# Two layers behind attention on one core: the tables of side work re-timed, product 5 ahead of the output pieces, weight fetches at a later unit, and an activation written with one relu

## The chip, the cores and the metric

The kernel runs on one core of a Trainium2 chip. A core has several engines, each with its own queue of instructions, taken strictly in order: TensorE (PE in the profile; PEld are its weight loads), VectorE (DVE), ScalarE (ACT), GpSimd (POOL) and SyncE (SP, which here only issues DMA transfers). Engines wait for one another by semaphores. The metric is the device time of one execution in microseconds (us).

## The reference

Causal attention with a decay feeds a feed-forward layer whose activation is h * relu6(h + 3) / 6, and that one a second layer whose activation is a PReLU with a slope per column:

```python
decay = cum[:, :, :, None] - cum[:, :, None, :]          # cum: running sum of log f
scores = where(causal, -1e9, scale * (q @ k.T) + decay)
attn = softmax(scores) @ v                                # 4 x 8 heads, 576 tokens, head width 64
x = attn as 2304 tokens x 512
h = x @ w_in;  g = h * clip(h + 3, 0, 6) / 6;  x = g @ w_out          # 512 -> 2048 -> 512
h = x @ w_in;  g = max(h, 0) + alpha * min(h, 0);  out = g @ w_out    # the same sizes
```

The weights reach the kernel as 64-bit words, and are converted to 32-bit floats on the chip.

## The kernel before

**Start and attention.** 32 heads are worked off as 16 pairs. For each head a tile of q and k (`rqk`) is loaded, prepared (`prep_head`, `prep_low`: high and low halves) and completed by four added rows that carry the decay. For the first two heads these rows are made in place; for the others they go through DRAM: `aq_d` and `ak_d` are stored once, and `prep_head` loads four rows of each (L313, L314). Attention runs to about 214 us. Beside it the weights of the first group are converted: `fetch` (L117) loads raw words, and the steps `m`, `f`, `s`, `j`, `g` (L137 to L153, ACT and DVE) make floats of them.

**The two layers.** The work is cut into 48 sets: two layers, in each 8 groups of 256 hidden columns by 3 blocks of 768 tokens. A set is a 2 x 2 block product done as in Strassen's and Winograd's schemes, with seven products (numbered 1 to 7) in place of eight. A product is six matmuls of 128 x 384 (high and low halves). Products accumulate in three PSUM banks: 1, 6, 7 and 4 one after another in bank A (tile `hA`), 5 and 3 in C (`hC`), 2 in B (`hB`). Behind products 1, 6 and 5 ACT copies the bank out (`keep`, L705); the next product of that bank must wait for it. Behind 3, 7 and 2 DVE adds the bank to such a copy (`add`, L708). Then `activate`: `first` on ACT (L663 in layer one; L666 and L668 in layer two), `second` on DVE (L674, L677), `third` a cast to the high half on ACT (L682) and the low half on POOL (L683). The activated blocks of a set are multiplied by the second weight matrix in the *pieces* (L731 in layer one, L733 in layer two), which run during the next set; DVE or ACT adds a piece's result (L740, L751, L738, L749).

**The order.** `run` walks a string for each set: a digit is a product, `q` one piece of the set before. Each character is a *unit*, and all engines' instructions are written out in the order of units: what `later` puts down for a unit comes right behind its matmuls, then what `aside` puts down. Side work has due units: `conversion` reads a table of names and units (`S1` to `S4` are sums of weight blocks on POOL, L167; `ha` to `hd` and `ho` casts on ACT, L181; `la` to `ld` and `lo` low halves on POOL, L185), and `build` makes the input blocks of the next sets (sums L237, casts L240, low halves L245), evenly spread if a rate is given.

Of the kernel before, what the change touches and what calls it, by code (L numbers as in the profile page):

```python
# [8 lines left out]
F32 = mybir.dt.float32  # L9
# [12 lines left out]
def decay_attention_ffn2_kernel(ctx, tc, qk, v, f, wi1, wo1, wi2, wo2, alpha, out):  # L22
# [28 lines left out]
    CONV_EVEN = "m0 0 f0 1 s0 2 j0 3.5 g0 5 m1 4 f1 6.5 s1 8 j1 9 g1 10 S1 11 S2 12 S3 12 hc 13 ha 13 lc 14 hb 14 la 15 lb 16 S4 17 m2 18 hd 18 f2 19 ld 19 s2 20 j2 21 m3 21 g2 22.5 f3 23 ho0 23 lo0 24 s3 24.5 j3 26 g3 27 ho1 28 lo1 29 wi0 40 wi1 43 wo0 46 wo1 48"  # L51
    CONV_TURN = "p0 0 p1 0 S1 6 S2 7 S3 7 hc 8 ha 8 lc 9 hb 9 la 10 lb 11 S4 12 hd 13 ld 14 p2 14 p3 15 ho0 24 lo0 25 ho1 26 lo1 27 wi0 40 wi1 43 wo0 46 wo1 48"
# [225 lines left out]
    def attention():  # L278
        with ExitStack() as ax:
# [219 lines left out]
            aug_consts(1)  # L499
            make_identity(nc, identb)  # L500
# [3 lines left out]
            nc.gpsimd.memset(aq.bitcast(F32)[:, :, 512:640], 0.0)  # L504
            nc.gpsimd.memset(aq.bitcast(F32)[:, 2:4, 0:512], -1.0)
            nc.gpsimd.memset(ak[:, 0:2, :].bitcast(F32), 1.0)
# [15 lines left out]
            prep_head(1)  # L522
            prep_low(1)
# [3 lines left out]
            for a in range(2):  # L527
                nc.gpsimd.affine_select(out=maskj[64 * a:64 * a + 64], in_=maskj[64 * a:64 * a + 64],
                                        pattern=[[-1, TAIL]], compare_op=ALU.is_ge,
                                        fill=-1.0e9, base=0, channel_multiplier=1)  # L530
            scaled("P", aq[:, 0:2, 0:512], hl[:, :, 0:512].bitcast(F32))
# [5 lines left out]
            nc.gpsimd.tensor_scalar(out=alpha_sb, in0=alpha_sb, scalar1=-1.0, scalar2=None, op0=ALU.mult)  # L537
# [9 lines left out]
            def aside(t, *fns):  # L547
                side.setdefault(t, []).extend(fns)

            aside(2, lambda: fetch(0), lambda: fetch(1))  # L550
# [64 lines left out]
    SEQ = ("1qq5q6q3q7q2q4q", "1q5q6q3q7q2q4")  # L615
    FIRST = ("152637..4", "15qq6qq3q7q2q4q", "1qq5qq6q3q7q2q4")
# [37 lines left out]
    def activate(s, gt, i, n, h, d):  # L654
# [5 lines left out]
        def first():  # L660
# [6 lines left out]
            hold["g"] = g32 = P["tp"].tile([128, NB], F32, tag="t", name="t") if (i, n) == (1, 0) else h()  # L667
            nc.scalar.activation(out=g32, in_=h(), func=AF.Relu)  # L668
            hold["t"] = t

        def second():
# [3 lines left out]
            else:  # L675
                m = g * FT + i
                nc.vector.scalar_tensor_tensor(out=g32, in0=hold["t"], scalar=alpha_sb[:, m:m + 1], in1=g32,  # L677
# [11 lines left out]
    def product(s, c, gt, k):  # L689
# [24 lines left out]
        else:  # L714
            k2, i, n = {2: (1, 0, 0), 7: (5, 1, 1), 3: (6, 0, 1)}[k]
            later(0, lambda: add(k2))
# [40 lines left out]
    def side_work(s):  # L757
# [13 lines left out]
        if s == (0, 1, 0):  # L771
            conversion(early["first"], CONV_FIRST, True)
            build(1, 1, both, even=(1, 1.5))
        if s == (0, 0, 1):
            ops = conv_ops(0, 2)
            conversion(ops, CONV_A, True, 1, 1)
# [126 lines left out]
```

## Time and profile before

| what | value |
|---|---|
| runs | 1013.03 us median of 3 (1013.02 to 1017.4) |
| profiled execution, its own time | 1012.13 us |
| its span | 1010.3 us |
| PE busy | 965.5 us, 96% of the span, 5488 matmuls |
| DVE, ACT, POOL busy | 735.9, 589.1, 590.0 us |

The span is what the profiler saw of that execution; the time of the execution is 1.8 us more. Busy shares are means over parts with different limits, so the stretch in question is looked at below, and the waits of PE.

### The profile page before, as it was taken

The page shows a single profiled execution, that of the slowest core. Times are in us where ns is not written, and L with a number is a line of the kernel's source. Part 1 is how long each engine was busy: PE and PEld are TensorE (multiplying, and loading weights), DVE is VectorE, ACT ScalarE, POOL GpSimd, SP SyncE. Part 2 cuts the span into 40 slices and gives each one's busy share as a digit, 9 for nine tenths or more (in the row PEclk, how much of TensorE's full clock was granted, in tenths as well). Part 3 has the DMA queues.
Part 4 walks back from the last instruction along what each step waited for, and adds up shares of the span by engine and source line. Part 5 has one row for each costly group of instructions (what it writes and reads, how often), then busy time and mean ns, then how long its engine had stood idle before and what let it go on. Part 6 is the DMA issues. An engine that isn't in the chain of part 4 may idle for free.

```text
span 1010.3 us, 15919 instructions
## 1 busy us (share of the span) xinstructions
PE 965.5 (96%) x5488; PEld 859.7 (85%) x5488; DVE 735.9 (73%) x1284; ACT 589.1 (58%) x1444; POOL 590.0 (58%) x577
## 2 busy tenths in 40 slices
PE   4999999999999999999999989999999999999998
PEld 3767666678899999998998988789898888898997
DVE  6888988857698788878989846145687788735454
ACT  5677787776555555555654445665565656564452
POOL 8567568956646666566485269566556556532222
PEclk9999999999999999999999999999999999999999
DMA  6555576501424444310576851332344420243531
GB/s 219 174 173 168 176 239 208 150 2 42 156 66 177 178 175 169 107 48 1 198 308 241 308 184 48 137 129 81 125 160 168 166 84 1 104 182 142 229 150 68
DMA packets 36868, 147.57 MB, mean 146 GB/s; under 512 B 4668, under 2 KB 4668, under 8 KB 33652
## 3 DMA queue, kind: packets, MB, share of 16 engines
q1 hardware_dynamic: 36784, 146.56, 41.7%
q8 instruction: 43, 0.70, 0.3%
q14 instruction: 37, 0.30, 0.1%
q10 hardware_dynamic: 4, 0.00, 0.0%
HBM read 98.26 MB, written 44.14 MB: 141 GB/s over the span
## 4 chain that ended last, share of the span: by engine, by line
PE 57%; DVE 23%; POOL 7%; ACT 6%; issue 4%; DMA 2%; SPq 0%; POOLq 0%; ACTq 0%; DVEq 0%
PE o L733 13%; PE hA L700 12%; PE o L731 12%; PE hC L700 7%; PE pv L454 4%; PE hB L700 3%; DVE nm L341 3%; PE tp L397 2%; DVE t L674 2%; PE sc L364 2%; POOL wi L185 2%; POOL g L683 1%; DVE r L751 1%; DVE s L708 1%; ACT g L682 1%
## 5 line engine op out<-in xcount | busy, mean ns | idle before, releaser
L731 PE MATMUL o<-g,wo 128*128 128x384 f32 x1152 | 233.3, 341 | 2.0 <-POOL g L683 2.0
L700 PE MATMUL hA<-xh,wi 128*128 128x384 f32 x768 | 225.8, 339 | 9.0 <-ACT s L705 5.4
L733 PE MATMUL o<-wo,g 128*128 128x512 f32 x864 | 225.5, 395 | 4.0 <-POOL g L683 3.0
L683 POOL TENSOR_TENSOR g<-t,g 128x384 fp32r<-128x384 f32 x120 | 128.8, 1073 | 156.1 <-ACT g L682 134.6
L731 PEld LDWEIGHTS o<-g,wo 128*128 128x128 f32 x1152 | 205.6, 189 | 4.6 <-POOL g L683 3.3
L733 PEld LDWEIGHTS o<-wo,g 128*128 128x128 f32 x864 | 159.8, 188 | 33.2 <-POOL g L683 6.2
L683 POOL TENSOR_TENSOR g<-s,g 128x384 fp32r<-128x384 f32 x72 | 74.7, 1038 | 155.6 <-ACT g L682 153.8
L700 PEld LDWEIGHTS hA<-xh,wi 128*128 128x128 f32 x768 | 142.0, 188 | 15.1 <-ACT s L705 7.6
L751 DVE TENSOR_TENSOR r<-o,r 128x512 f32<-128x512 f32 x126 | 86.2, 687 | 73.8 <-PE o L733 73.7
L700 PE MATMUL hA<-xl,wi 128*128 128x384 f32 x384 | 129.7, 338 | 0.0
L682 ACT CAST g<-t 128x384 fp32r<-128x384 f32 x120 | 61.9, 515 | 113.0 <-DVE t L674 97.3
L700 PE MATMUL hC<-xh,wi 128*128 128x384 f32 x384 | 115.0, 340 | 3.6 <-ACT s L705 3.6
L740 DVE SCALAR_TENSOR_TENSOR r<-o,r 128x384 f32<-128x384 f32 x168 | 90.6, 549 | 21.2 <-PE o L731 21.0
L349 ACT ACTIVATE p<-sc,nm 128x128 f32<-128x128 f32 (+4 forms) x160 | 84.6, 532 | 22.9 <-DVE nm L341 10.9
L245 POOL TENSOR_TENSOR xl<-r,xh 128x384 fp32r<-128x384 f32 x65 | 78.5, 1225 | 4.1 <-ACT xh L240 3.7
L341 DVE TENSOR_REDUCE nm<-sc 128x1 f32<-128x128 f32 (+4 forms) x160 | 71.7, 470 | 10.1 <-PE sc L366 8.5
L700 PEld LDWEIGHTS hC<-xh,wi 128*128 128x128 f32 x384 | 71.3, 189 | 6.7 <-ACT s L705 4.6
L700 PEld LDWEIGHTS hA<-xl,wi 128*128 128x128 f32 x384 | 72.4, 189 | 3.1
L682 ACT CAST g<-s 128x384 fp32r<-128x384 f32 x72 | 37.1, 515 | 60.1 <-DVE s L677 53.4
L397 PE MATMUL tp<-ident,p 128*128 128x128 f32 x384 | 68.6, 282 | 0.6 <-ACT pt L413 0.6
L364 PE MATMUL sc<-k,q 128*128 128x256 f32 (+2 forms) x128 | 55.6, 434 | 11.9 <-DVE k L332 9.8
L700 PE MATMUL hC<-xl,wi 128*128 128x384 f32 x192 | 65.1, 339 | 0.0
(128 smaller groups left out, 1901.8 us busy)
## 6 DMA issues: line engine op xcount, KB each, us to landing
wid<-wi SPq DMA_DIRECT2D x24, 896.0 KB
wi<-wid SPq DMA_DIRECT2D x12, 1792.0 KB
rqk<-in_qk SPq DMA_DIRECT2D x32, 608.0 KB
raw<-in_wi SPq DMA_DIRECT2D x32, 512.0 KB
raw<-in_wo SPq DMA_DIRECT2D x32, 512.0 KB
wod<-wo SPq DMA_DIRECT2D x24, 512.0 KB
wo<-wod SPq DMA_DIRECT2D x12, 1024.0 KB
vt<-in_v SPq DMA_DIRECT2D x16, 320.0 KB
```

What stands on the lines that cost most here:

```text
L245: e.tensor_sub(out=XS[k][1][:, b, c], in0=x, in1=XS[k][0][:, b, c].bitcast(F32))
L341: nc.vector.tensor_reduce(out=nm[:, i:i + 1], in_=src, axis=AX.X, op=ALU.max, negate=True)
L349: nc.scalar.activation(out=pt[:, c0:c0 + cw], in_=src, func=AF.Exp, bias=nm[:, 0:1], scale=1.0, accum_out=dsts[i])
L364: nc.tensor.matmul(out=sc[:, 0:n], lhsT=q1[:, qs], rhs=k1[:, 0:n], start=True, stop=False)
L397: nc.tensor.transpose(tp[:, j, :], pt[:, 128 * j:128 * j + 128], ident)
L682: nc.scalar.copy(out=gt[n][i][:, 0], in_=hold["g"])
L683: nc.gpsimd.tensor_sub(out=gt[n][i][:, 1], in0=hold["g"], in1=gt[n][i][:, 0].bitcast(F32))
L700: nc.tensor.matmul(out=h, lhsT=a, rhs=b[:, x, kc], start=new and kc + e == 0, stop=kc == KH - 1 and e == 2, skip_group_check=not new)
L731: nc.tensor.matmul(out=o[:, 0:NB], lhsT=a[:, cs], rhs=b, start=st, stop=sp)
L733: nc.tensor.matmul(out=o, lhsT=b[:, cs], rhs=a, start=st, stop=sp)
L740: later(0, lambda: nc.vector.scalar_tensor_tensor(out=acc, in0=o[:, 0:NB], scalar=1.0 / 6.0, in1=acc, op0=ALU.mult, op1=ALU.add))
L751: nc.vector.tensor_add(out=acc, in0=o, in1=acc)
```

## The change

It has six parts. The tables `CONV_EVEN` and `CONV_TURN` get other units (the cast `hb`, which needs no sum, first, the other casts behind the sums they read), and the set (0, 0, 1) uses `CONV_EVEN` stretched by 1.1 instead of two other tables. At the start three memsets are written earlier and the preparation of head 1 later. The first two raw fetches move from unit 2 of the attention to units 8 and 10. In the strings product 5 comes in front of the output pieces that follow product 1. `add` goes to the front of its unit's list, ahead of activations. In layer two `first` makes only relu(-h), and `second` computes h + (1 - alpha) * relu(-h), which is the same function; `alpha_sb` holds 1 - alpha.

```diff
-    CONV_EVEN = "m0 0 f0 1 s0 2 j0 3.5 g0 5 m1 4 f1 6.5 s1 8 j1 9 g1 10 S1 11 S2 12 S3 12 hc 13 ha 13 lc 14 hb 14 la 15 lb 16 S4 17 m2 18 hd 18 f2 19 ld 19 s2 20 j2 21 m3 21 g2 22.5 f3 23 ho0 23 lo0 24 s3 24.5 j3 26 g3 27 ho1 28 lo1 29 wi0 40 wi1 43 wo0 46 wo1 48"
-    CONV_TURN = "p0 0 p1 0 S1 6 S2 7 S3 7 hc 8 ha 8 lc 9 hb 9 la 10 lb 11 S4 12 hd 13 ld 14 p2 14 p3 15 ho0 24 lo0 25 ho1 26 lo1 27 wi0 40 wi1 43 wo0 46 wo1 48"
+    CONV_EVEN = "m0 0 f0 1.5 s0 2.5 j0 4 g0 5 m1 4 f1 6.5 s1 8 j1 9 g1 10 S1 11 S2 12 S3 13 hb 13 hc 14.5 lb 15 ha 15.5 lc 16 la 17 S4 18 m2 19 hd 20 f2 20.5 ld 21 s2 21.5 j2 22.5 m3 22 g2 23.5 f3 24 s3 25 ho0 25.5 j3 26.5 lo0 27 g3 27.5 ho1 28.8 lo1 29.6 wi0 40 wi1 43 wo0 46 wo1 48"
+    CONV_TURN = "p0 0 p1 0 S1 5 S2 6 S3 7 hb 8 hc 9 lb 10 ha 10.5 lc 11 la 12 S4 13 hd 15 p2 15 ld 16 p3 18 ho0 24 lo0 25.5 ho1 26 lo1 27 wi0 40 wi1 43 wo0 46 wo1 48"
...
+            nc.gpsimd.memset(aq.bitcast(F32)[:, :, 512:640], 0.0)
+            nc.gpsimd.memset(aq.bitcast(F32)[:, 2:4, 0:512], -1.0)
+            nc.gpsimd.memset(ak[:, 0:2, :].bitcast(F32), 1.0)
             make_identity(nc, identb)
...
-            nc.gpsimd.memset(aq.bitcast(F32)[:, :, 512:640], 0.0)
-            nc.gpsimd.memset(aq.bitcast(F32)[:, 2:4, 0:512], -1.0)
-            nc.gpsimd.memset(ak[:, 0:2, :].bitcast(F32), 1.0)
...
             load_head(3)
-            prep_head(1)
-            prep_low(1)
             nc.gpsimd.memset(three, 3.0)
...
+            prep_head(1)
+            prep_low(1)
             scaled("P", aq[:, 0:2, 0:512], hl[:, :, 0:512].bitcast(F32))
...
-            nc.gpsimd.tensor_scalar(out=alpha_sb, in0=alpha_sb, scalar1=-1.0, scalar2=None, op0=ALU.mult)
+            nc.gpsimd.tensor_scalar(out=alpha_sb, in0=alpha_sb, scalar1=-1.0, scalar2=1.0, op0=ALU.mult, op1=ALU.add)
...
-            aside(2, lambda: fetch(0), lambda: fetch(1))
+            aside(8, lambda: fetch(0))
+            aside(10, lambda: fetch(1))
...
-    SEQ = ("1qq5q6q3q7q2q4q", "1q5q6q3q7q2q4")
-    FIRST = ("152637..4", "15qq6qq3q7q2q4q", "1qq5qq6q3q7q2q4")
+    SEQ = ("15qq6qq3q7q2q4q", "15q6qq3q7q2q4")
+    FIRST = ("152637..4", "15qq6qq3q7q2q4q", "1qqqq5q6qq372q4")
...
             nc.scalar.activation(out=t, in_=h(), func=AF.Relu, scale=-1.0)
-            hold["g"] = g32 = P["tp"].tile([128, NB], F32, tag="t", name="t") if (i, n) == (1, 0) else h()
-            nc.scalar.activation(out=g32, in_=h(), func=AF.Relu)
-            hold["t"] = t
+            hold["g"] = t
...
-                nc.vector.scalar_tensor_tensor(out=g32, in0=hold["t"], scalar=alpha_sb[:, m:m + 1], in1=g32,
+                nc.vector.scalar_tensor_tensor(out=g32, in0=g32, scalar=alpha_sb[:, m:m + 1], in1=h(),
                                                op0=ALU.mult, op1=ALU.add)
...
-            later(0, lambda: add(k2))
+            at.setdefault(now[0], []).insert(0, lambda: add(k2))
...
-            build(1, 1, both, even=(1, 1.5))
+            build(1, 1, both, even=(1, 1.3))
...
-            conversion(ops, CONV_A, True, 1, 1)
-            conversion(ops, CONV_B, True, 1, 4, 0, 25)
-            conversion(ops, CONV_B, True, 1, 7, 25)
+            conversion(ops, CONV_EVEN, True, 1.1, 2)
```

Three places show how the order of instructions moves. A row names the line, the operation, what is written and what is read.

SP at the start, the difference of the two orders: `aq_d` is the store of the added rows of q, `raw` the raw weight words, the tiles `q_` and `k_` the added rows of heads 2 and 3, `rqk` and `vt` the loads of head 4.

```order
 L536 DMA aq_d<-aq 16x2560 x2
-L117 DMA raw<-in_wi 128x512 x2
-L313 DMA q_279<-aq_d 4x640
-L314 DMA k_281<-ak_d 4x576
-L313 DMA q_345<-aq_d 4x640
-L314 DMA k_347<-ak_d 4x576
-L295 DMA rqk<-in_qk 128x1216
-L300 DMA vt<-in_v 128x640
+L313 DMA q_275<-aq_d 4x640
+L314 DMA k_277<-ak_d 4x576
...
+L300 DMA vt<-in_v 128x640
+L117 DMA raw<-in_wi 128x512 x2
```

The two raw fetches stand behind the rows of heads 2 and 3 and the loads of head 4.

DVE in the second set of layer one, before: `hC`, `hA` and `hB` are the sums behind products 3, 7 and 2.

```order
L148 SCALAR_TENSOR_TENSOR wb<-raw,wb 128x512
L153 SCALAR_TENSOR_TENSOR wb<-raw,wb 128x512
L245 TENSOR_TENSOR xl_3592<-r_81,xh_3591 128x384
L708 TENSOR_TENSOR s<-hC,s 128x384
L245 TENSOR_TENSOR xl_3592<-r_81,xh_3591 128x384
L674 SCALAR_TENSOR_TENSOR t<-t,s 128x384
L708 TENSOR_TENSOR s<-hA,s 128x384
L237 TENSOR_TENSOR r_81<-r_81 128x384 x3
L674 SCALAR_TENSOR_TENSOR t<-t,s 128x384
L708 TENSOR_TENSOR s<-hB,s 128x384
```

The same place in the changed kernel, where `add` is on L707 and `second` on L673:

```order
L148 SCALAR_TENSOR_TENSOR wb<-raw,wb 128x512
L153 SCALAR_TENSOR_TENSOR wb<-raw,wb 128x512
L245 TENSOR_TENSOR xl_3592<-r_81,xh_3591 128x384
L707 TENSOR_TENSOR s<-hC,s 128x384
L707 TENSOR_TENSOR s<-hA,s 128x384
L673 SCALAR_TENSOR_TENSOR t<-t,s 128x384
L245 TENSOR_TENSOR xl_3592<-r_81,xh_3591 128x384
L237 TENSOR_TENSOR r_81<-r_81 128x384
L707 TENSOR_TENSOR s<-hB,s 128x384
L673 SCALAR_TENSOR_TENSOR t<-t,s 128x384
```

The sum of `hA` moved ahead of a low half (L245) and an activation.

ACT in the last set of layer one, before: the tiles `wi` are casts of the first weights of layer two, `xh_` those of input blocks, and L705 the copies.

```order
L705 COPY s<-hA 128x384
L181 CAST wi<-wc 128x2x256
L181 CAST wi<-wa 128x2x256
L181 CAST wi<-wb 128x2x256
L240 CAST xh_78<-r_81 128x384 x2
L705 COPY s<-hC 128x384
L705 COPY s<-hA 128x384
```

The same place in the changed kernel, with the copies on L704:

```order
L704 COPY s<-hA 128x384
L181 CAST wi<-wb 128x2x256
L704 COPY s<-hC 128x384
L181 CAST wi<-wc 128x2x256
L181 CAST wi<-wa 128x2x256
L240 CAST xh_78<-r_81 128x384 x2
L704 COPY s<-hA 128x384
```

The copy of product 5 moved ahead of two casts that read POOL's sums and of the two input casts; the cast of `wb`, which reads no sum, moved to the front.

## Rows read from the trace of the kernel before

**Rows 1.** PE's waits, whole span: engine, line, releaser: us in total, times, longest.

```profile
PE sc L365 <- DMA k<-ak_d: 3.9, 1, 3.9
```

**Rows 2.** PE's waits from 236 to 265 us.

```profile
PE hA L700 <- DVE s L708: 2.1, 1, 2.1
PE hA L700 <- ACT g L682: 1.4, 1, 1.4
```

**Rows 3.** PE's waits from 265 to 592 us.

```profile
PE hA L700 <- ACT s L705: 2.2, 2, 1.6
PE o L731 <- POOL g L683: 2.0, 4, 0.6
```

**Rows 4.** PE's waits from 592 to 640 us.

```profile
PE hC L700 <- ACT s L705: 3.1, 2, 2.6
PE hA L700 <- ACT s L705: 2.9, 3, 1.3
PE o L733 <- POOL g L683: 1.2, 1, 1.2
```

**Rows 5.** Groups of instructions, 645 to 1000 us: busy, mean ns, idle before and releasers.

```profile
L733 PE MATMUL o<-wo,g 128*128 128x512 f32 x802 | 210.0, 395 | 2.8 <-POOL g L683 1.8 <-ACT g L682 1.0
```

**Rows 6.** Busy time by stretch: PE, PEld, DVE, ACT, POOL, clock, DMA share, GB/s.

```profile
240.00:245.00 5.00, 2.90 (x14) 2.58 (x13) 4.88 (x6) 2.45 (x6) 3.45 (x3) 0.88 0.33 105
245.00:250.00 5.00, 5.00 (x24) 5.00 (x23) 3.64 (x7) 3.38 (x8) 2.42 (x3) 0.78 0.00 0
...
240.00:265.00 25.00, 21.49 (x113) 20.88 (x112) 22.52 (x35) 13.32 (x29) 15.38 (x13) 0.93 0.13 44
300.00:350.00 50.00, 50.00 (x287) 50.00 (x286) 40.28 (x72) 27.00 (x53) 33.78 (x33) 1.00 0.49 179
592.00:640.50 48.50, 41.27 (x211) 38.21 (x210) 22.81 (x37) 26.05 (x55) 44.33 (x42) 0.96 0.18 64
```

**Rows 7.** Timeline of the start: start, us, engine, line, idle before and releaser.

```profile
0.74 0.59 SPq L471 DMA_DIRECT2D fl<-in_f  x1
...
3.35 1.39 DVE L507 TENSOR_SCALAR fl<-fl 64x576 f32<-64x576 f32 x1 [0.18 <-DMA fl<-in_f]
...
16.34 2.86 SPq L117 DMA_DIRECT2D raw<-in_wi  x2
...
20.73 0.29 SPq L314 DMA_DIRECT2D k<-ak_d  x1
...
25.06 0.35 PE L365 MATMUL sc<-k,q 68*128 68x256 f32 x1 [3.86 <-DMA k<-ak_d]
```

**Rows 8.** Timeline of DVE ahead of the wait at 243 us.

```profile
241.39 1.34 DVE L674 SCALAR_TENSOR_TENSOR t<-t,s 128x384 f32<-128x384 f32 x1
242.66 0.55 DVE L708 TENSOR_TENSOR s<-hA,s 128x384 f32<-128x384 f32 x1
```

**Rows 9.** Copy of product 1 and first matmul of product 6, two sets.

```profile
285.93 0.47 ACT L705 COPY s<-hA 128x384 f32<-128x384 f32 x1
...
286.52 0.37 PE L700 MATMUL hA<-xh,wi 128*128 128x384 f32 x1
...
526.38 0.47 ACT L705 COPY s<-hA 128x384 f32<-128x384 f32 x1
...
527.71 0.34 PE L700 MATMUL hA<-xh,wi 128*128 128x384 f32 x1
```

**Rows 10.** Timeline from 592 us: POOL's first weight sum, ACT's first weight cast.

```profile
592.96 0.74 POOL L167 TENSOR_TENSOR wc<-wa,wb 128x256 f32<-128x256 f32 x1 [3.88 <-issue]
...
595.41 0.62 ACT L181 CAST wi<-wc 128x512 fp32r<-128x512 f32 x1 [5.37 <-POOL wc L167]
```

**Rows 11.** Timeline of one set of layer two: second relu, copy, product 6.

```profile
772.88 0.53 ACT L668 ACTIVATE s<-s 128x384 f32<-128x384 f32 x1
...
775.81 0.49 ACT L705 COPY s<-hA 128x384 f32<-128x384 f32 x1
...
777.06 0.34 PE L700 MATMUL hA<-xh,wi 128*128 128x384 f32 x1
```

## The prediction

> **What bounds the kernel now.** I read the busy times by stretch first. In a plain stretch of layer one, 300 to 350 us, PE is busy for 50.00 of 50 us with 287 instructions, which is 0.174 us a matmul and 1.05 us for a product or a piece of six; DVE does 40.28 there, ACT 27.00 and POOL 33.78 [rows 6]. So PE sets the pace, and the change, which takes no matmul away, can win only where PE stands still. I therefore went to the list of what PE waits for, first over the whole span and then by stretch. The reader is to see five places. At the start one wait of 3.9 us for the DMA that brings the added rows of k for the second head [rows 1]. Between 236 and 265 us, the second and third set of layer one, two waits of 2.1 and 1.4 us [rows 2]. Between 265 and 592 us, 20 sets, small ones: 2.2 us for copies of bank A and 2.0 us for the low halves that POOL makes for the output pieces [rows 3]. Between 592 and 640 us, where layer two begins, 3.1, 2.9 and 1.2 us [rows 4]. After that 2.8 us in all before output pieces, over some 22 sets [rows 5].
>
> A long wait costs twice. After the 2.1 us wait the granted clock of 240 to 245 us is 0.88 and of 245 to 250 us 0.78: 0.12 and 0.22 of 5 us, 1.7 us lost at the lower level (1.2 GHz). Over all of 240 to 265 us it is 0.93, which is 1.75 us lost, so nothing more was lost after the 1.4 us wait [rows 6]. A wait of 1.4 us left the clock alone here, and one of 2.1 us did not; where between them it turns these rows don't say. From 592 to 640.5 us it is 0.96, 1.9 us lost, which I put to the longest wait there, 2.6 us [rows 4, 6]. I charge 1.7 us to each of the waits of 3.9, 2.1 and 2.6 us.
>
> **Start.** PE stops at 21.20 us (25.06 less 3.86) and goes on when the rows of k have landed. SP issued them at 20.73 us, 4.3 us earlier, behind two raw fetches of 512 KB each, issued from 16.34 us on [rows 7]. The change puts these fetches behind the rows of q and k. A small transfer that nothing stood ahead of, fl at 0.74 us, was there for DVE at 3.35 us, 2.6 us later [rows 7]. So k lands at 23.3 us instead of 25.0, and the wait becomes 2.1 us: **-1.7 us**. That is the length after which the clock fell at 243 us, so I take no clock back. The bounds: nothing, if heads 2 and 3 fill the queues anyway, and -5.6 us (3.86 and the clock). The moved memsets and the first head's preparation change the order on POOL, but not the sum of what stands ahead of the store of aq there; so I leave that store's landing, which SP waits for before it issues the rows, where it is.
>
> The Trainium skill, page "DMA: Bandwidth & Descriptors", section "Anatomy of one DMA — SWDGE (gpsimd) path", gives a transfer a fixed cost of about 2.0 us whatever its size, on another issuing path than this one. By that rule (an estimate) the rows would land at 22.7 us, the wait would be 1.5 us and next to the 1.4 us after which the clock stayed, and this term would be -4.0 us. The trace has 2.6 us for 144 KB, and goes before it.
>
> **Second and third set.** PE's 2.1 us wait there is for the sum of product 7 on DVE, which started only at 242.66 us [rows 8], although its product was done before the piece ahead of the wait: it stood behind a low half (L245) and an activation (L674, at 241.39 for 1.34 us). In the change each sum stands at the head of its unit's list, and the even build is spread wider, so this sum follows the sum before it directly, and the low half and the activation come behind it; in the third set the join (L148) and the activation also give way. Both waits then go, 3.5 us, with 1.7 us of clock: 5.2 us at most. But DVE is busy for 22.52 of these 25 us [rows 6]. It cannot be compressed by more than the 2.5 us that it idles, except for work that slips behind 265 us, where it has room (40.28 of 50); I allow 1 us for that. **-3.5 us**, bounds -1.8 (the first wait is only shortened) and -5.2.
>
> **Remaining sets of layer one.** With product 5 ahead of the output pieces, the order 1, piece, piece, 5, piece, 6 becomes 1, 5, piece, piece, 6. A piece gets 1.05 us more for its low half to arrive, and all four waits of this kind (longest 0.6) go: -2.0 us. But product 6, which accumulates into bank A after product 1 has been copied out by ACT, comes one unit earlier after product 1. How much the copy leads was read set by set. In the tightest case the copy ends at 286.40 (285.93 and 0.47) and product 6 starts at 286.52, a lead of 0.12; in the last of six such sets it is 0.86 [rows 9]. In these six of 20 the lead is less than 1.05, and what is short adds up to 2.3 us. In the two sets where PE already waits for this copy (2.2 us, [rows 3]) the wait grows by a full unit each, 2.1 us. That is 4.4 us less 2.0. The sums in front bring the activations and casts ahead of the copy a little forward in some of them; I take **+2.0 us**, bounds -1 (copies all come earlier) and +4.5 (the piece waits had other causes).
>
> **Where layer two begins.** POOL is busy for 44.33 of the 48.5 us from 592 us [rows 6]. Its first sum of the new weights (L167) starts at 592.96 us with 3.88 us of idle time before it; ACT stands 5.37 us until POOL's second sum lets it cast at 595.41 us [rows 10], and behind three such casts stands the copy of product 5 for which PE waits 2.6 us. In the change one cast that needs no sum goes first, then that copy, then the others: this wait goes, with its clock 4.3 us, and the rest of [rows 4] is 4.6 us, so at most 8.9. But the weights are needed all the same, and POOL idles for only 4.2 us in that stretch, which is what this can shrink by unless POOL's work falls behind. I take **-3.0 us**, bounds 0 and -8.9.
>
> **Rest of layer two.** One ACT instruction of 0.53 us goes in each activation; DVE keeps its instruction, with h in place of the second relu as an input, so I cost it the same. Where the sum h comes straight from the PSUM bank the instruction reads PSUM, as the sums on DVE already do. Piece waits (2.8 us) go, as a product of 1.05 us comes in front of them. Here too product 6 moves up, by one piece. In the tight sets the copy, at 775.81 us, ends 0.76 before product 6 at 777.06 us; two of the removed instructions, one at 772.88 us of 0.53 us, stand ahead of it [rows 11], so that it moves up by 1.0 and product 6 by about 1.4: 0.4 of lead remain. I take **-2.5 us**, bounds 0 (the shorter ACT queue only idles and new copy waits eat the rest) and -2.8.
>
> **The sum.** -1.7 - 3.5 + 2.0 - 3.0 - 2.5 = -8.7 us. The profiled execution took 1012.13 us, the median of the runs is 0.9 us above that (1013.03), so 1003.4 becomes 1004.3; I say 1004.
>
> **Rivals.** *Slower: the sums in front hold DVE up.* A sum now waits at the head of DVE's queue for its product to end, and an activation of the unit before, which was ready, waits behind it; its cast, low half and piece follow late. With half a microsecond in each of the 38 sets without a wait that is +19 us, so 1023. It decides against the change from 0.18 us a set (8.7 over 48 sets). Against it: DVE has 9.7 us idle in 50 [rows 6], and pieces get 1.05 us more cover. Chance 0.08.
>
> *POOL gives it back.* The gain at 592 us comes out at nothing, since POOL ends its sums and low halves no earlier, and the copies in layer one cost their full 4.5: 1012.13 - 1.7 - 3.5 + 4.5 - 2.5 and the 0.9 is 1009.8; with only one of the two, 1007. For it: POOL's 44.33 of 48.5. Chance 0.20, of which 0.12 for a time within 0.5% of before.
>
> *The start does not change.* The heads' loads, not the raw fetches, keep the rows of k till 25 us: 1006. Chance 0.10.
>
> *Everything pays.* All waits and clock losses go (5.6, 5.2, 8.9, 2.8) and the copies cost nothing: 1012.13 - 22.5 + 0.9 is 990.5. With half of what lies between it and the sum, 997. Chance 0.15.
>
> The forecast itself has 0.47. A measurement of this kernel can tell about 0.5% (5 us) from no change. Faster by more: 0.47, 0.15, 0.10 and 0.08 of POOL's 0.20, 0.80; within it 0.12; slower 0.08. The range goes from between the two sizes of "everything pays", 994, to the worse of the POOL case, 1010.
>
> **What would show it.** Right: the wait for k at 21 us is 2.1 us and still followed by a low clock; no wait for a sum of product 7 at 243 us and a clock of 1.00 there; no 2.6 us wait at 598 us; no waits ahead of pieces, and more or longer waits of product 6 for ACT copies in layer one. Wrong: new waits in the plain sets (PE under 50 of 50 between 300 and 350 us), POOL behind at 640 us with waits that moved to its low halves, or an attention part that ends no earlier although its start did.

## The result, and the profile after

The changed kernel is slower: 1025.01 us median (1023.91 to 1026.77, 4 runs) against 1014.07 us (the three runs of before and a fourth), a ratio of 1.0104 (95% interval 1.0073 to 1.0134). The forecast was 1004 us. The profiled execution took 1025.94 us and its span is 1024.2 us, 13.9 us longer than that of before.

The parts of the two spans say where. The table takes the starts of the first matmul of product 1 of a set from the traces (sets numbered from 0; 24 begins layer two), and the difference of two starts is the length of a part:

| us | attention, to set 0 | sets 0 to 3 | 4 to 22 | 23 to 25 | 26 to 40 | rest |
|---|---|---|---|---|---|---|
| before | 214.5 | 66.7 | 307.0 | 57.7 | 241.6 | 122.7 |
| changed | 214.2 | 66.0 | 318.4 | 59.9 | 242.8 | 122.9 |
| difference | -0.4 | -0.7 | +11.4 | +2.2 | +1.2 | +0.2 |

Nearly all of the loss lies in the plain sets of layer one. PE's waits there, from 265 to 592 us, changed kernel (in total, times, longest):

```profile
PE hA L699 <- ACT s L704: 11.5, 11, 2.7
PE o L730 <- POOL g L682: 1.0, 2, 0.8
PE o L730 <- ACT g L681: 0.7, 1, 0.7
```

Against [rows 3] the waits for ACT's copies of bank A rose from 2.2 us in two places to 11.5 us in eleven; the waits ahead of pieces went from 2.0 to 1.7 us. Busy time by stretch, with the columns of [rows 6], in the changed kernel: first two stretches of 50 us, then two neighbouring sets.

```profile
300.00:350.00 50.00, 49.48 (x280) 48.70 (x279) 39.64 (x68) 25.45 (x51) 31.32 (x31) 1.00 0.45 169
350.00:400.00 50.00, 49.06 (x276) 47.88 (x275) 44.24 (x76) 25.14 (x50) 26.10 (x26) 1.00 0.37 132
...
313.77:330.39 16.62, 16.10 (x91) 15.78 (x91) 16.02 (x28) 8.54 (x18) 6.91 (x7) 1.00 0.22 77
330.39:346.43 16.04, 16.04 (x91) 15.79 (x91) 11.41 (x21) 7.88 (x17) 11.72 (x12) 1.00 0.61 232
```

Where PE was busy for all of 50 us, it now stands still for 0.5 to 0.9 us in 50, and executes 280 and 276 matmuls instead of 287. (7 to 11 matmuls are 1.2 to 1.9 us; why idle time comes out shorter than that is in the last section.) The sets alternate, and in every second one DVE is busy for 16.02 of 16.62 us. The same two sets before, in the same columns:

```profile
312.82:328.68 15.86, 15.86 (x92) 15.86 (x91) 15.14 (x27) 8.33 (x17) 7.20 (x7) 1.00 0.23 75
328.68:344.52 15.84, 15.84 (x91) 15.84 (x91) 11.40 (x22) 8.61 (x17) 12.56 (x13) 1.00 0.64 241
```

DVE had 0.7 us to spare in the first of the pair and 4.4 in the second; the 9.7 us in 50 of the prediction was a mean over both. The timeline of the changed kernel shows the wait itself, in the first of these sets (start, us, engine, line, what ended the idle time before):

```profile
316.40 0.58 ACT L664 ACTIVATE t<-hA,three 128x384 f32<-128x384 f32 x1
...
317.08 0.55 DVE L673 SCALAR_TENSOR_TENSOR t<-t,hA 128x384 f32<-128x384 f32 x1 [0.53 <-ACT t L664]
...
317.73 0.51 ACT L681 CAST g<-t 128x384 fp32r<-128x384 f32 x1 [0.74 <-DVE t L673]
...
318.14 0.47 ACT L704 COPY s<-hA 128x384 f32<-128x384 f32 x1
...
318.67 0.44 PE L699 MATMUL hA<-xh,wi 128*128 128x384 f32 x1 [0.52 <-ACT s L704]
```

Product 1 was over at 314.8 (it started at 313.77). ACT copies it out only at 318.14, since the cast of the last activation of the set before stands ahead of the copy, and that cast waits for DVE. Product 6, now three units behind product 1 instead of four, waits for the copy. The copy itself is later than it was: 3.3 us behind the end of product 1, where in the same set before it came 2.9 us behind it (312.82 and 1.05 us for product 1). The chain that ends in the copy was held up in the set before this one, where DVE stood idle at a sum for its product. ACT's casts and POOL's low halves come later in the set by that, and one low half now lies beside the whole of DVE's conversion L148, which stands ahead of the activations and takes 1.52 us instead of 1.06. DVE's sum and conversion in the changed kernel, then the conversion and the copy before:

```profile
308.71 0.56 DVE L707 TENSOR_TENSOR s<-hA,s 128x384 f32<-128x384 f32 x1 [0.48 <-PE hA L699]
...
313.96 1.52 DVE L148 SCALAR_TENSOR_TENSOR wc<-raw,wc 128x512 uint32<-128x512 uint32 x1
```

```profile
313.04 1.06 DVE L148 SCALAR_TENSOR_TENSOR wc<-raw,wc 128x512 uint32<-128x512 uint32 x1
...
316.77 0.48 ACT L705 COPY s<-hA 128x384 f32<-128x384 f32 x1
```

The clock had a part in it too. Behind the wait that ended at 467.6 us (2.4 us) it stood at its lower level for 3.4 us, which costs 1.7 us; before, it never fell in sets 4 to 22:

```profile
465.00:475.00 10.00, 7.62 (x35) 7.41 (x34) 8.96 (x14) 4.74 (x11) 7.54 (x7) 0.83 0.00 1
```

The start did what the change says. SP's rows and PE's waits for k, changed kernel:

```profile
20.66 0.24 SPq L314 DMA_DIRECT2D k<-ak_d  x1
...
22.51 0.90 SPq L117 DMA_DIRECT2D raw<-in_wi  x2
...
26.89 0.54 SPq L326 DMA_DIRECT2D k<-k  x1
...
22.34 0.36 PE L365 MATMUL sc<-k,q 68*128 68x256 f32 x1 [1.55 <-DMA k<-ak_d]
...
34.95 0.36 PE L365 MATMUL sc<-k,q 68*128 68x256 f32 x1 [1.12 <-DMA k<-k]
```

The rows landed 1.7 us after their issue, not 4.3 [rows 7]. But most of that was given back: PE is 4.2 us ahead of before at 29 us and 0.3 us at 50 us. A later load of k, issued at 26.89 us, comes only at 35 us; the raw fetches that were moved had been issued 4.4 us ahead of it (no run shows whether they are what delayed it). From 30 to 45 us PE is busy for 12.20 of 15 us at a granted clock of 0.89, where it had 14.85 at 1.00 before (the lower level of the clock lay at 25 to 30 us then, with a mean of 0.66). Where layer two begins, the waits of [rows 4] were replaced by others. From 592 to 640 us, changed kernel:

```profile
PE hA L699 <- ACT s L704: 1.5, 1, 1.5
PE o L730 <- ACT g L681: 1.5, 1, 1.5
PE o L730 <- POOL g L682: 0.6, 1, 0.6
```

In sets 23 to 25 PE stands still for as long as before (7.0 and 7.2 us), but the clock is lower, before and changed:

```profile
588.28:645.97 57.69, 50.45 (x259) 46.88 (x259) 26.93 (x44) 32.04 (x68) 46.97 (x45) 0.97 0.28 99
```

```profile
598.60:658.53 59.93, 52.92 (x259) 48.76 (x259) 28.49 (x46) 29.78 (x63) 46.19 (x45) 0.91 0.31 106
```

A mean of 0.97 loses 1.7 us here, one of 0.91 some 5 us; the difference alone is more than the 2.2 us by which this part grew. And from 640 us on, where waits for copies took the place of the piece waits of [rows 5] (the 2.1 us lies at 641 us, still in set 25):

```profile
PE hA L699 <- ACT s L704: 5.1, 9, 1.2
PE o L732 <- POOL g L682: 2.1, 1, 2.1
```

### The profile page after: what moved, and what is told of

Its sections match the earlier page's. It is cut to its first block, busy times and chain, and to the rows that moved or that the text cites. A ratio compares the mean times of both kernels' runs of the same rounds, so it can differ in the third digit from the quotient of the medians.

```text
span 1024.2 us, 15848 instructions
## 1 busy us (share of the span) xinstructions
PE 972.0 (95%) x5488; PEld 860.1 (84%) x5488; DVE 750.6 (73%) x1284; ACT 535.8 (52%) x1348; POOL 584.7 (57%) x577
## 5 line engine op out<-in xcount | busy, mean ns | idle before, releaser
L682 POOL TENSOR_TENSOR g<-t,g 128x384 fp32r<-128x384 f32 x192 | 201.9, 1052 | 332.1 <-ACT g L681 324.8
L699 PE MATMUL hA<-xh,wi 128*128 128x384 f32 x768 | 228.8, 343 | 19.3 <-ACT s L704 18.6
L730 PE MATMUL o<-g,wo 128*128 128x384 f32 x1152 | 230.6, 342 | 5.8 <-POOL g L682 3.0
L732 PE MATMUL o<-wo,g 128*128 128x512 f32 x864 | 222.0, 397 | 2.1 <-POOL g L682 2.1
L681 ACT CAST g<-t 128x384 fp32r<-128x384 f32 x192 | 98.6, 514 | 229.6 <-DVE t L676 114.9
L732 PEld LDWEIGHTS o<-wo,g 128*128 128x128 f32 x864 | 162.0, 190 | 31.5 <-POOL g L682 3.7
L750 DVE TENSOR_TENSOR r<-o,r 128x512 f32<-128x512 f32 x126 | 86.6, 688 | 67.0 <-PE o L732 66.8
L245 POOL TENSOR_TENSOR xl<-r,xh 128x384 fp32r<-128x384 f32 x65 | 76.9, 1201 | 5.6 <-ACT xh L240 5.3
L667 ACT ACTIVATE t<-s 128x384 f32<-128x384 f32 x72 | 37.6, 523 | 58.8 <-DVE s L707 58.8
L676 DVE SCALAR_TENSOR_TENSOR t<-t,alpha_sb,s 128x384 f32<-128x384 f32 x72 | 59.0, 819 | 8.3 <-ACT t L667 7.2
L664 ACT ACTIVATE t<-s,three 128x384 f32<-128x384 f32 x72 | 44.0, 611 | 39.3 <-DVE s L707 39.3
```

What stands on the lines that cost most here:

```text
L245: e.tensor_sub(out=XS[k][1][:, b, c], in0=x, in1=XS[k][0][:, b, c].bitcast(F32))
L676: nc.vector.scalar_tensor_tensor(out=g32, in0=g32, scalar=alpha_sb[:, m:m + 1], in1=h(), op0=ALU.mult, op1=ALU.add)
L681: nc.scalar.copy(out=gt[n][i][:, 0], in_=hold["g"])
L682: nc.gpsimd.tensor_sub(out=gt[n][i][:, 1], in0=hold["g"], in1=gt[n][i][:, 0].bitcast(F32))
L699: nc.tensor.matmul(out=h, lhsT=a, rhs=b[:, x, kc], start=new and kc + e == 0, stop=kc == KH - 1 and e == 2, skip_group_check=not new)
L730: nc.tensor.matmul(out=o[:, 0:NB], lhsT=a[:, cs], rhs=b, start=st, stop=sp)
```

## Experiments

Theory 1: time is lost because product 6 comes a unit sooner and ACT's copy of product 1 stands behind a cast that waits for DVE. Theory 2, the rival: the sums at the head of DVE's queue make the copies late. The columns of the tables are the parts above, from each run's profile, one profile a run. The run with the first table alone, further below, tells how far one profile can be trusted: it differs from before only from 740 us on, and its parts up to there are 217.1, 66.7, 306.7 and 59.0 us, against 214.5, 66.7, 307.0 and 57.7. So a difference below some 3 us in the attention part, or below some 1.3 us in sets 23 to 25, is no sign of an effect.

**Undoing one part of the change at a time, and moving the cast.** The strings of before, else as changed:

```diff
-    SEQ = ("15qq6qq3q7q2q4q", "15q6qq3q7q2q4")
-    FIRST = ("152637..4", "15qq6qq3q7q2q4q", "1qqqq5q6qq372q4")
+    SEQ = ("1qq5q6q3q7q2q4q", "1q5q6q3q7q2q4")
+    FIRST = ("152637..4", "15qq6qq3q7q2q4q", "1qq5qq6q3q7q2q4")
```

> The changed kernel with the strings of before (product 5 behind the output pieces again), all else as changed. Theory 1 (product 6 comes one unit sooner behind product 1 and waits for ACT's copy, which stands behind a cast that waits for DVE): the 18.6 us of waits for copies of bank A fall to about 5, some 3 us of waits ahead of pieces return, time about 1012. Theory 2 (the sums at the head of DVE's queue make the copies late): the copies stay late, and time stays at 1019 or above.

The sums behind the activations again:

```diff
-            at.setdefault(now[0], []).insert(0, lambda: add(k2))
+            later(0, lambda: add(k2))
```

> The changed kernel with the sums back behind the activations of their unit, all else as changed. Theory 2: the copies come as early as before, and the waits before product 6 nearly go, about 1013. Theory 1: the copy leads by what it led before less one unit, which is short in a few sets only by 2 to 4 us in all plus the waits that grow; 1019 to 1024.

The changed kernel with the cast and the low half behind products 2 and 4 one unit later:

```diff
-    def activate(s, gt, i, n, h, d):
+    def activate(s, gt, i, n, h, d, wait=0):
...
-        later(d + 1, third)
+        later(d + 1 + wait, third)
...
-            activate(s, gt, 1, 0, lambda: h, 0)
+            activate(s, gt, 1, 0, lambda: h, 0, 1)
...
-            activate(s, gt, i, n, lambda: c[k2], 1)
+            activate(s, gt, i, n, lambda: c[k2], 1, 1 if k == 2 else 0)
```

> The changed kernel with the last cast (and low half) of the activations behind products 2 and 4 one unit later, so that in ACT's queue the copy of product 1 stands ahead of them. Theory 1: the waits for copies of bank A fall from 18.6 to under 4 us, and the time by 14 us or more, to 1011 or below. Theory 2: what makes the copy late stands on DVE ahead of the activation too, so the waits fall by less than half, 1019 or above.

And the kernel before with nothing but the new strings (the first diff the other way round):

> The kernel before with the new strings alone. Theory 1: waits for copies grow by 5 to 10 us, less 3 us of piece waits, 1016 to 1022. Theory 2: only the two sets that wait already grow, 1013 to 1015.

| run | median us | ratio to before (95%) | attention | 0 to 3 | 4 to 22 | 23 to 25 | 26 to 40 |
|---|---|---|---|---|---|---|---|
| old strings | 1023.74 | 1.0080 (1.0055 to 1.0105) | 211.6 | 68.8 | 312.6 | 61.2 | 245.5 |
| sums back | 1017.53 | 1.0035 (1.0019 to 1.0050) | 211.2 | 66.2 | 316.5 | 57.8 | 240.1 |
| cast later | 1009.36 | 0.9947 (0.9928 to 0.9966) | 212.9 | 65.6 | 305.7 | 59.9 | 240.0 |
| before, new strings | 1023.66 | 1.0077 (1.0050 to 1.0103) | 217.9 | 66.7 | 315.3 | 60.4 | 240.0 |

The time with the old strings came out as theory 2 had it, those with the cast later and with the new strings alone as theory 1 had it, and the one with the sums back as neither. Neither theory holds alone. The strings cost 8.3 us in sets 4 to 22 by themselves (315.3 less 307.0), and without them 5.6 us stay (312.6). Of the 8.3 us, 3.4 are the clock, which fell behind two waits. The kernel before with the new strings, PE's waits in sets 4 to 22 and two stretches of 5 us behind the waits:

```profile
PE hA L700 <- ACT s L705: 9.4, 5, 3.7
```

```profile
470.00:475.00 5.00, 5.00 (x21) 5.00 (x20) 4.00 (x6) 2.98 (x8) 4.92 (x5) 0.66 0.00 0
555.00:560.00 5.00, 4.99 (x20) 4.99 (x21) 4.41 (x7) 2.79 (x6) 4.43 (x4) 0.66 0.99 353
```

But the run with the cast later took both away: 305.7 us, less than before. PE's waits in that run from 285 to 592 us:

```profile
PE hA L699 <- DMA wi<-wid: 1.0, 3, 0.5
PE hA L699 <- ACT s L704: 0.7, 1, 0.7
PE o L730 <- POOL g L682: 0.5, 1, 0.5
PE hA L699 <- DVE s L707: 0.3, 1, 0.3
```

Of some 11.5 us of waits for copies 0.7 is left, with the sums still in front and product 5 still ahead of the pieces. The 1009.36 us also beat the kernel before.

**Each other part alone, on the kernel before.** The sums in front (the second diff the other way round):

> The kernel before with the sums at the head of their unit's list alone. If the sums in front by themselves make the copies late, as the run with the old strings suggests (5.6 us lost between the sixth and the twenty-fourth set), waits for copies and pieces grow and the time is 1016 to 1021. If they only cost together with something else of the change (the tables, the activation), 1012 to 1015.

The tables: the two lines of the diff of the change, the set (0, 0, 1) and the even rate.

> The kernel before with the new tables alone (the two conversion tables, the set that now uses the first of them, the build spread wider). By the prediction's step on the place where layer two begins: the 2.6 us wait goes, 1009 to 1012. If POOL gives it back there: 1012 to 1016, with new waits before 660 us that add up to what went.

The activation of layer two: the three places of the diff of the change.

> The kernel before with the activation of layer two alone (one relu less). If the shorter ACT queue brings the low halves forward: the 2.8 us of piece waits after 645 us fall by half or more, 1010 to 1012. If ACT only idles: within 1 us of before.

And, the other way about, the changed kernel with the cast later and the sums back (the second and third diff together):

> The changed kernel with the last casts behind products 2 and 4 one unit later and the sums back behind the activations. If the cast ahead of the copy was the whole way by which both parts cost time, this is within 2 us of the run with the casts later alone (1009.4). If the sums in front cost something else besides, it is faster by 2 us or more; if they pay once the copy is free, slower by as much.

| run | median us | ratio to before (95%) | attention | 0 to 3 | 4 to 22 | 23 to 25 | 26 to 40 |
|---|---|---|---|---|---|---|---|
| before, sums in front | 1024.34 | 1.0111 (1.0085 to 1.0137) | 215.3 | 67.5 | 313.1 | 59.6 | 244.5 |
| before, tables | 1019.74 | 1.0054 (1.0033 to 1.0075) | 217.3 | 67.8 | 307.3 | 58.8 | 244.9 |
| before, activation | 1007.59 | 0.9938 (0.9923 to 0.9953) | 215.3 | 66.8 | 306.5 | 57.9 | 236.7 |
| cast later, sums back | 1002.95 | 0.9892 (0.9867 to 0.9916) | 213.8 | 65.1 | 305.3 | 60.2 | 236.8 |

The times with the sums and with the tables came out above both of their expectations, the one with the activation below its own. The sums in front alone cost as much as the whole change: 6.1 us in layer one, 1.9 where layer two begins (1.7 of it the clock, at a mean of 0.94 instead of 0.97), 2.9 in sets 26 to 40. But in layer one, with the old strings, it is not the waits for copies that grew. PE's waits in sets 4 to 22, with the sums alone and before:

```profile
PE o L731 <- POOL g L683: 2.0, 6, 0.6
PE hA L700 <- ACT s L705: 1.7, 5, 0.6
PE o L731 <- ACT g L682: 1.0, 2, 0.6
```

```profile
PE hA L700 <- ACT s L705: 2.2, 2, 1.6
PE o L731 <- POOL g L683: 1.6, 3, 0.6
```

The whole lists, with smaller rows, have 5.5 us against 4.2, which is 1.3 of the 6.1 us; the rest are delays too short for them. If one takes for every matmul how much later than 0.175 us after the one before it starts, the delays ahead of and within pieces add up to 7.6 us, against 3.0 before, and those of products to 5.2, against 3.7. So here it is mostly the pieces that wait, for casts and low halves that come late. The tables cost 3.3 us in sets 26 to 40, and gain nowhere. The activation is the part that pays: 4.9 us in sets 26 to 40. The group of piece matmuls there, from 660 to 1010 us in its run (columns of [rows 5]), waits for nothing any more:

```profile
L731 PE MATMUL o<-wo,g 128*128 128x512 f32 x798 | 206.4, 395 | 0.0
```

The last run is 6.4 us faster than the one with the cast later alone (some 5.6 us by the ratios to before), so the sums in front cost something besides: in sets 26 to 40 it is 3.2 us, even with the cast later (240.0 against 236.8).

**Does the cast explain the sums too?** The kernel before with the sums in front and the cast later (third diff):

> The kernel before with the sums in front and the last casts behind products 2 and 4 one unit later, nothing else. If the sums in front cost time because ACT's copies then stand behind a cast that waits for DVE, most of the 11 us of the run with the sums in front alone come back: 1016 or below. If they cost it on DVE itself, where every second set keeps DVE busy for 15.1 of 15.9 us, 1020 or above.

And three versions around the best: without the tables, without the strings too, and with only the table of layer two's beginning as before:

```diff
-            conversion(ops, CONV_EVEN, True, 1.1, 2)
+            conversion(ops, CONV_A, True, 1, 1)
+            conversion(ops, CONV_B, True, 1, 4, 0, 25)
+            conversion(ops, CONV_B, True, 1, 7, 25)
```

> New strings, the activation, the later fetches and the later casts; sums behind the activations, tables of before. If the new tables cost here what they cost alone (6 us): 995 to 999. If their cost is gone once the copy leads: 1001 to 1005.

> The same with the strings of before as well: the activation, later fetches and later casts alone. If product 5 ahead of the pieces pays once the copy is free, 2 to 5 us more than the run with the new strings; if the strings are worth nothing, the same within 1 us; if they still cost, less.

> The changed kernel with casts later and sums behind the activations, and with the table used where layer two begins as before. If that table is what loses between 592 and 660 us (2.5 us there in the run that it is compared with): 1000 to 1001. If the loss there has another cause: 1002 to 1005.

| run | median us | ratio to before (95%) | attention | 0 to 3 | 4 to 22 | 23 to 25 | 26 to 40 |
|---|---|---|---|---|---|---|---|
| before, sums in front, cast later | 1015.90 | 1.0020 (1.0006 to 1.0034) | 217.0 | 66.8 | 305.6 | 59.3 | 243.0 |
| no tables | 1005.42 | 0.9905 (0.9891 to 0.9920) | 212.9 | 65.8 | 304.3 | 61.2 | 236.3 |
| no tables, old strings | 1003.08 | 0.9880 (0.9863 to 0.9896) | 213.1 | 66.1 | 303.5 | 59.6 | 236.8 |
| old table where layer two begins | 1004.80 | 0.9903 (0.9886 to 0.9919) | 212.6 | 65.1 | 304.7 | 62.1 | 236.8 |

With the cast later, the sums in front cost little in layer one (305.6, where they alone had 313.1, and where the third of these runs, with the later cast and without them, has 303.5): there it was mostly ACT's queue, not DVE's time. How late the copy of product 1 comes says the same. From the end of product 1 (1.05 us after its start) to the start of its copy it is on average over sets 4 to 22, in us: before 2.9, new strings alone 2.8, sums in front alone 3.7, whole change 3.4, change with the sums back 2.9, change with the cast later 1.7, sums in front with the cast later 1.5. The strings leave the copies where they were and bring product 6 a unit closer to them; the sums make the copies later; the later cast brings them forward. In layer two 1.4 us of cost stay. The expectation that the tables' 6 us would come off again (995 to 999) missed: without the tables it is no faster. So did the one on the table of layer two's beginning: with the old one sets 23 to 25 take 62.1 us instead of 60.2, so the new one loses nothing there (that it gains is little more than one profile can tell). The version with the activation, the changes at the start and the later cast, and everything else as before, is as fast as any other here: product 5 ahead of the pieces, the sums in front and the tables together buy nothing.

**Where layer two begins.** All of these versions take 57 to 62 us for sets 23 to 25. Is POOL the bound? The eight sums of input blocks that POOL makes there were given to DVE, in the changed kernel and in the version with the activation, fetches and cast alone:

```diff
-                build(0, 1, (nc.gpsimd, nc.vector), nc.gpsimd)
+                build(0, 1, (nc.gpsimd, nc.vector), nc.vector)
```

> The changed kernel, with the eight sums of input blocks that POOL makes where layer two begins (about 1.1 us each) made by DVE, which is half idle there. If POOL bounds that stretch: the three sets from the last of layer one on take 52 to 56 us instead of 59.9, and the time is 4 to 8 us less than that of the changed kernel. If the waits there come from ACT's order or the weights' arrival: within 2 us.

> The activation, the later fetches and the later casts with everything else as before (1003.1), and the same eight sums on DVE. If POOL bounds the stretch: 995 to 999. If not: 1002 to 1005.

And the first table alone on the kernel before (its line in the diff of the change):

> The kernel before with the new first conversion table alone, used by the conversions of layer two between 740 and 890 us only. If the 3.3 us that the run with all tables lost there come from this table: 1016 to 1018, with piece waits above 4 us after 660 us. If they come from work put off by the other tables: within 1 us of before.

They took 1024.43 us (ratio to before 1.0096, 1.0079 to 1.0113), 1003.67 (0.9893, 0.9876 to 0.9911) and 1016.99 (1.0026, 1.0013 to 1.0039). Sets 23 to 25 took 58.2 us (1.7 less than changed) and 60.5 (0.9 more than the version it is compared with), although POOL is busy there for some 39 instead of 46 us. Neither difference is more than that of the clock: in the first run its mean there is 0.94 instead of 0.91, in the second 0.94 instead of 0.97, 1.7 us each. So POOL's work is not the bound. The first table is where the tables, put alone on the kernel before, lose in layer two: 244.5 us in sets 26 to 40, with PE waiting there for casts and low halves (from 660 us on):

```profile
PE o L733 <- ACT g L682: 2.5, 4, 0.8
PE o L733 <- POOL g L683: 1.8, 4, 0.7
```

The timeline of the changed kernel showed what POOL's first sum (L167) waits for. SP and POOL, changed kernel:

```profile
590.94 0.43 SPq L195 DMA_DIRECT2D fd<-wa  x1
...
599.14 0.32 SPq L197 DMA_DIRECT2D wa<-fd  x1
599.51 0.52 SPq L197 DMA_DIRECT2D wb<-fd  x1
...
603.82 0.74 POOL L167 TENSOR_TENSOR wc<-wa,wb 128x256 f32<-128x256 f32 x1 [5.45 <-issue]
```

The blocks for the sum are reloaded from DRAM (wa and wb). Their load stands on SP until the store before it (fd<-wa) has landed, and the sum starts 4.3 us after the second load was issued. The list of SP's waits from 590 to 606 us has it:

```profile
SPq L197 <- DMA fd<-wa: 7.8, 1, 7.8
```

The store itself was issued behind 2.8 MB of weight loads (two, of 1024 and 1792 KB). To bring it ahead of them, the last four saved conversions were spaced 4 units apart instead of 6:

```diff
-                        aside(6 * k + (0, 1, 2, 3, 4, 5)[i], ops[f"{name}{k % 4}"])
+                        aside(6 * k - 2 * max(0, k - 11) + (0, 1, 2, 3, 4, 5)[i], ops[f"{name}{k % 4}"])
```

once on the version without tables and strings, once with both:

> The activation, the later fetches and the later casts (1003.1), and the last four conversions that are saved to DRAM in the sixth to the second set before layer two begins spaced 4 units apart instead of 6, so that the last store stands ahead of the weight loads of 2.8 MB in SP's queue. If the arrival of the reloaded blocks, which waits for that store, is what makes POOL's first sum late: the sum starts 4 us or more sooner after its set begins, the 3.8 us wait for the copy in bank C goes, 996 to 1000. If ACT's order or POOL's work set it: 1001 to 1005.

> The same with the new strings and tables (1003.0 without it). If the new table where layer two begins could not pay for want of the blocks: 995 to 999, and below the run with the old ones. If it is worth nothing: the same as that run or 1001 to 1005.

They took 1008.15 us (0.9937, 0.9915 to 0.9959) and 1008.32 us (0.9941, 0.9918 to 0.9965), slower than without the edit and outside their expectations, but the stretch is shorter, 53.5 and 54.2 us instead of 59.6 and 60.2. Sets 23 to 25 of the first, and those of the version that it is compared with:

```profile
593.02:646.52 53.50, 48.51 (x260) 45.44 (x260) 29.18 (x45) 29.45 (x62) 46.47 (x44) 1.00 0.27 96
```

```profile
582.70:642.27 59.57, 50.70 (x260) 46.80 (x259) 28.86 (x45) 29.50 (x62) 46.94 (x45) 0.97 0.28 97
```

POOL's first sum now starts 1.3 us ahead of set 23, where it came 5.8 us behind its start. With the blocks there in time, PE's idle time falls from 8.9 to 5.0 us, and the clock stays at 1.00. The loss came earlier: sets 4 to 22 took 313.7 us instead of 303.5. ACT and PE in that run, ahead of it, and the stretch from 569 us:

```profile
571.48 0.66 ACT L137 ACTIVATE wa<-raw 128x512 f32<-128x512 f32 x1 [8.78 <-DMA raw<-in_wo]
...
573.75 0.69 PE L699 MATMUL hA<-xh,wi 128*128 128x384 f32 x1 [6.51 <-DVE s L707]
```

```profile
569.00:579.00 10.00, 5.25 (x22) 5.25 (x23) 6.75 (x13) 4.48 (x9) 2.36 (x3) 0.66 0.48 175
```

The conversion that was moved forward now waits on ACT for its raw words, and DVE, and the sum that PE needs, wait behind it: 6.5 us, and 3.4 us more at the lower level of the clock, which together are nearly the 10.2 us. Whether a version with both mended is faster was not tried.

## Why the prediction was wrong

**Start, -1.7 us forecast.** The mechanism was right, and the wait at 22 us fell further than forecast, to 1.6 us instead of 2.1: the rows landed 1.7 us after issue, not the 2.6 us taken from fl. The Trainium skill's fixed cost of about 2.0 us ("DMA: Bandwidth & Descriptors", section "Anatomy of one DMA — SWDGE (gpsimd) path") came closer than my row; this case's trace, with 1.7 us, is below it. Nor did the clock fall behind this wait, as the forecast had it; it fell at 42 us. In this pair of profiles only 0.4 us is left at the end of attention. But the same attention code ran in 19 profiles: with the start as before set 0 began at 214.5 to 217.9 us (7 profiles, mean 216.4), with the changed start at 211.2 to 214.9 (12, mean 213.0). The changes at the start (fetches, memsets and the preparation of head 1, which no run separates) are worth 3.3 us on average; one profile each could not show it.

**Second and third set, -3.5.** The 2.1 us wait went, and set 2 began 3.5 us sooner than before, 0.4 of it from attention. Then sets 2 and 3 took 36.8 us instead of 34.4, and set 4 began only 1.1 us sooner. DVE's lack of room, which that step named as the limit, is not what took it back: in these two sets of the changed kernel DVE is busy for 25.17 of 36.83 us. PE waits there for casts, low halves and sums by turns; no run here separates them.

**Remaining sets of layer one, +2.0: the step that failed**, with +11.4 measured. Two terms of it were wrong, that of the strings and that of the sums. I counted the copies' leads set by set and found 4.4 us short, but took the leads of before as fixed. In the kernel before with the new strings alone the part grew by 8.3 us, so the strings' term itself was mis-sized by a factor of four. Of this, 3.4 us are the clock behind the waits of 3.7 and 2.6 us: I let a wait of 1.6 us grow past the 2.1 us for which I charged the clock elsewhere, and put the clock at nothing. The two waits that were there before (1.62 and 0.56 us) also grew by 2.05 us each, not by one unit of 1.05, since the piece waits that I took as gone stood ahead of them in the same sets, and PE now comes to the copy sooner by these too. And the sums in front, which I let bring the copies forward, made them later (2.9 us behind product 1 on average before, 3.7 with the sums alone): the lag of the copy in the set of the timeline shown is 3.3 us from the end of product 1 to its start, against 3.15 us (three units) until product 6 is due. The later-cast runs show the place: a cast ahead of the copy in ACT's queue, waiting for DVE. DVE in turn stands longer at sums for their products: 3.6 us in sets 4 to 22 before, 6.2 with the sums alone. The prediction's own sign of being wrong, PE under 50 of 50 us between 300 and 350 us, is what came (49.48).

**The slower rival** named the sums in front, and its point of decision, 0.18 us a set, was passed: 8.7 us would do for 48 sets, and they alone cost about 11 us. Its path, cast, low half and piece, is the one that the sums alone take in layer one with the old strings. In the whole change, with product 5 ahead of the pieces, what waits there is product 6, for the copies (11.5 us of waits, against 1.7 ahead of pieces); and the strings, which this rival left out, cost 8.3 us there by themselves. That the time came out near its 1023 us is in part luck. And what I held against it, 9.7 us of idle DVE in 50, averaged a set with 0.7 us to spare with one that has 4.4. That mean is why I gave it 0.08.

**Where layer two begins, -3.0**, with +2.2 measured. The step counted on less waiting and a higher clock. PE waited as long as before (7.0 and 7.2 us), in other places, and the clock cost some 5 us instead of 1.7. The rival "POOL gives it back" described the waiting, but taking eight sums away from POOL changed little. What was late is the reload from DRAM behind the store; [rows 10] had it as 3.88 us of idle time before POOL's first sum, which I read as slack of POOL and not as a wait for a transfer.

**Rest of layer two, -2.5**, with +1.2 measured. The activation alone is worth 4.9 us, above my bound of 2.8: the bound held only the listed waits, and the sets with such waits were longer than these (see the last section). What ate it in the whole change are waits for copies of bank A, as in layer one (the 5.1 us above less 1.2 in set 25; before, there were none). With the sums back the part takes 240.1 us, with the cast later 240.0, with both 236.8. The sums in front were costed at nothing there. The first table's cost alone (+2.9) does not carry over: with the cast later and the sums back the part is 236.8 us with the tables and 236.3 without.

## What to carry to other kernels

When an instruction is moved closer to the one that it depends on through another engine, read what stands ahead of the producer in that engine's queue and what that in turn waits for; a lead measured before the change holds only while those queues keep their order. Read an engine's room set by set, not over a stretch that mixes full and half-empty ones. And of a bundle, time each part alone: here one part (the activation) gained 0.6%, two lost 0.8 and 1.1% and a third 0.5%, and moving two casts of each set by a unit, with their low halves, took more than the whole loss in layer one away.

## What the hardware showed beyond that

A wait's length did not settle whether the clock fell: in the changed kernel, the stretch from 30 to 45 us, with no listed wait above 1.4 us, had a mean granted clock of 0.89, while the stretch around the 1.4 us wait of [rows 2] lost none. In the same kernel a wait of 2.38 us, which ended at 467.6 us, was followed by 3.4 us at the lower level, and one of 2.65 us, which ended at 554.6 us, by none:

```profile
552.00:562.00 10.00, 7.41 (x42) 7.41 (x43) 8.85 (x15) 5.04 (x11) 6.74 (x6) 1.00 0.79 295
```

So the prediction's charge of 1.7 us for a wait of 2.1 us or more is right in some places and wrong in others. And short waits cost more than the list says: the set from 313.77 us is 0.76 us longer than its like before, with 0.52 us of listed wait. In the profile a matmul of 384 columns takes 0.34 us and two in a row 0.51, so each starts some 0.17 us before the one ahead of it ends. The list counts from that end, and so leaves 0.17 us out of every wait (0.52 and 0.17 are 0.69 of the 0.76 us), and the shortest waits altogether.

Work on POOL went with longer instructions on DVE. In the kernel before and in the changed one none of DVE's conversions of L148 and L153 that had no POOL instruction beside it took more than 0.69 us. Of those that had, some took no longer and others up to 1.9 us; many took about 0.55 us more than the time for which POOL ran beside them (1.52 us with 0.97 us, 1.06 with 0.51). No run separates this from other causes, but it is a way by which an order on ACT and POOL changes how much time DVE has.
